# w_down in three loads, two of them into the first 64 partitions, and in front of wo's first half

## The chip, the cores and the metric

The kernel runs on one core of one Trainium2 chip. The time is the device time of one execution in microseconds; a version's time is the median of its runs. Beside it stands one profiled execution, whose trace gives the start and duration of every instruction and the traffic of the 16 DMA engines.

## The reference

One decode step of a gated mixture of two branches, in float32, for a batch of 4 with one token each and a model width of 512:

```python
g = sigmoid((x * gate_w).sum(-1, keepdims=True))
q = (x @ wq) as [4, 32 heads, 128]
p = softmax(q . k_cache / sqrt(128)) over 4096 cached positions
a = (p . v_cache) as [4, 1, 4096] @ wo
b = (gelu(x @ w_gate) * (x @ w_up)) @ w_down
return g * a + (1 - g) * b
```

The caches are [4, 32, 4096, 128] each, 268 MB apiece. The weights are wq [512, 4096], wo [4096, 512], w_gate and w_up [512, 1792], and w_down [1792, 512]. All of it is read once; the output is 8 KB.

## The kernel before, in words

**Attention.** The 128 pairs of batch and head are taken in 32 steps of four heads of one batch entry (`NT`, `HT`). A step's k is one load of 128 partitions by 64 KB, 8.4 MB: a head lies on 32 partitions, each with 128 positions. VectorE (DVE in the profile) multiplies it by the query (`products`, L213) and adds up over the head's width (`sums`, L219), each in a quarter and a three-quarter part. The softmax's maximum goes over TensorE (PE) and ScalarE (ACT) (`max_a`, `soft_max`), and PE multiplies the weights by v in 32 products (`pv`, L272). `gather_a`, `gather`, `weigh`, `turn` and `turned` bring the results of 16 heads into the form that the product with wo wants. wo is used in two halves of 16 heads: the first half's attention is done in the middle of the run, the second's after the last step.

**The feed-forward branch** runs up to its hidden layer at the start (`ffn_up`, `ffn_gelu`, while k's first load is worked on). Its 1792 hidden values are turned into `hT` by 14 transposes (L349), one for each row of w_down that a partition holds: partition p holds the rows 14 p to 14 p + 13, and product i takes row i of all partitions.

**One tile for all that is loaded.** `big` has 45,056 numbers on each of 128 partitions; `place(a, n)` is a piece of it. Two k places overlap by a quarter, and the v place follows them at `VA`. The last v (`V(31)`) is put at 0, into the place of the last but one k. When the steps are over, wo's first half goes to `W0`, the first half of the v place, w_down to `D0`, the second half of it, and wo's second half to `W1`, inside the last k's place. At `ES`, behind wo's second half, small tiles for the last products follow; the last k's place ends 4096 numbers behind `ES`.

**The order.** The program is written in order by hand and each engine takes its instructions in that order. All loads are issued by SyncE (SP) in one queue. SP waits for a load's place to be free: for v's place until `pv` has read it, for k's until `sums` has. A load that waits holds up those behind it in SP's order. Each load counts up one of eight semaphores, which are used in turn. The last loads are, in order: k of step 31, v of step 30, v of step 31, wo's first half (4 MB), w_down (3.5 MB), and wo's second half in four pieces of 9, 4, 2 and 1 sixteenths (`WO_END`).

**The tail.** After the last `pv`, PE multiplies with wo's first half: 16 products into `wide` (`project_wide`, L254), which has four groups of 32 partitions, the products taken in turn; then the 16 transposes of the second half's attention (`turn(1)`, L307) and w_down's 14 products into `wide`. `fold` copies `wide` (ACT, L264) and adds its four groups into `acc`; wo's second half is multiplied into `acc` by 64 products (`project`, L259), four for each sixteenth. `res` is copied from `acc` and stored (L413, L414).

Of the kernel before, what the change touches and what calls it, by code (L numbers as in the profile page):

```python
# [9 lines left out]
F32 = mybir.dt.float32  # L10
# [7 lines left out]
def tile_gated_mix(ctx: ExitStack, tc: tile.TileContext, x, kc, vc, wq, wo, w_gate, w_up, w_down, gate_w, out):  # L18
    nc = tc.nc
    P = 128  # L20
    B, H, S, D = kc.shape
    DM = x.shape[2]
    F = w_gate.shape[1]
# [9 lines left out]
    RJ = 4  # L33
    BP = 2
    FG = F // 4
    FC = F // P
    HW = 16
    E = HW * D // P
    GW = HW // HT
    WO_END = (0, 9, 13, 15, E)  # L40
    scale = 1.0 / math.sqrt(D)
    c_gelu = math.sqrt(2.0 / math.pi)

# [8 lines left out]
    consts = ctx.enter_context(tc.tile_pool(name="consts", bufs=1))  # L52
# [9 lines left out]
    big = kv.tile([P, VA + TW], F32)  # L62
    Q0, F0, F1, W0, D0 = VA, VA, VA + KC * F, VA, VA + TW // 2
    W1, ES = TW, TW + TW // 2

    def place(a, n):
        return big[:, a:a + n]
# [10 lines left out]
    def load_k(i):  # L78
        load_kv(kc, i, K(i))

    def load_v(i):
        load_kv(vc, i, V(i))

    def load_f(s):
        nc.sync.dma_start(place((F0, F1)[s], KC * F), (w_gate, w_up)[s].rearrange("(p c) n -> p (c n)", c=KC))

    def load_d():
        nc.sync.dma_start(place(D0, FC * DM), w_down.rearrange("(p i) n -> p (i n)", i=FC))

    def load_w(w):  # L90
        t = place((W0, W1)[w], E * DM)
        src = wo[w * HW * D:(w + 1) * HW * D].rearrange("(p e) n -> p (e n)", e=E)
        ends = WO_END if w else (0, E)
        for e0, e1 in zip(ends, ends[1:]):
            nc.sync.dma_start(t[:, e0 * DM:e1 * DM], src[:, e0 * DM:e1 * DM])

# [41 lines left out]
    def gates():  # L138
        z = ps2.tile([P, 1], F32, name="sm")
        for c in range(KC):  # L140
            nc.tensor.matmul(z, xT[:, c, :], gw[:, c:c + 1], start=c == 0, stop=c == KC - 1)
        g1 = gate(z)
        z = ps2.tile([P, B], F32, name="sm")
        for c in range(KC):
            nc.tensor.matmul(z, gw[:, c:c + 1].to_broadcast([P, P]), xT[:, c, :32:8], start=c == 0, stop=c == KC - 1)
        g4 = gate(z)

        half = consts.tile([P, 1], F32)
        nc.vector.tensor_scalar(half, g1, -0.5, 0.5, op0=OP.mult, op1=OP.add)
        gmask = consts.tile([P, B, HT], F32)  # L150
        nc.vector.tensor_tensor(gmask, g4[:, :, None].to_broadcast([P, B, HT]), pmask[:, None, :].to_broadcast([P, B, HT]),
                                op=OP.mult)
        return half, gmask
# [5 lines left out]
    for c in range(KC):  # L159
        w = place(Q0 + c * H * D, H * D)  # L160
# [31 lines left out]
    def q_spread(g):  # L192
        ps = ps1.tile([P, B, D], F32, name="q")
        for h in range(HT):
            j, a = divmod(HT * g + h, HG)
            nc.tensor.matmul(ps[h * PH:(h + 1) * PH].rearrange("p b d -> p (b d)"),  # L196
                             hmask[:, j, a:a + 1].to_broadcast([P, PH]), QM.rearrange("p b d -> p (b d)"),
                             start=True, stop=True)
        QB[g] = work.tile([P, B, D], F32, name="qb")
        nc.scalar.activation(QB[g], ps, AF.Copy)  # L200
# [8 lines left out]
    def products(i, shared):  # L209
        g, b = divmod(i, B)  # L210
        r0, r1 = rows(i, shared)
        t = K(i).rearrange("p (r d) -> p r d", d=D)[:, r0:r1]
        nc.vector.tensor_tensor(t, t, QB[g][:, b:b + 1, :].to_broadcast([P, r1 - r0, D]), op=OP.mult)  # L213

    def sums(i, shared):
        if shared:
            SC[i] = work.tile([P, R], F32, name="sc")
        r0, r1 = rows(i, shared)
        nc.vector.tensor_reduce(SC[i][:, r0:r1], K(i).rearrange("p (r d) -> p r d", d=D)[:, r0:r1], axis=AX.X, op=OP.add)  # L219
# [10 lines left out]
    def soft_max(i):  # L230
        g, b = divmod(i, B)
        m2 = work.tile([1, HT], F32, name="m2")
        nc.vector.tensor_reduce(m2, MT[i].rearrange("o (h p) -> o h p", h=HT), axis=AX.X, op=OP.max)  # L233
        nbp = ps2.tile([P, HT], F32, name="sm")
        nc.tensor.matmul(nbp, ones[:1, :], m2, start=True, stop=True)  # L235
        nb = work.tile([P, HT], F32, name="nb")
        nc.scalar.activation(nb, nbp, AF.Copy, scale=-scale)  # L237
        for h in range(HT):
            s = slice(h * PH, (h + 1) * PH)
            nc.scalar.activation(PM[:, PZ:].rearrange("p (c m) -> p c m", m=32)[s, :, h:RJ * HT:HT],  # L240
                                 SC[i][s, :].rearrange("p (c j) -> p c j", j=RJ), AF.Exp, bias=nb[s, h:h + 1], scale=scale,
                                 accum_out=RS[g % 2][s, b, h:h + 1])
# [1 line left out]

    acc = ps1.tile([P, C4], F32, name="acc")
    wide = ps1.tile([P, DM], F32, name="wide")
    NW = FC + E
    nw = iter(range(NW))


    def project_wide(t, w):
        n = next(nw)
        c = n % 4
        nc.tensor.matmul(wide[32 * c:32 * c + 32, :], t, w, start=n < 4, stop=n >= NW - 4)  # L254

# [6 lines left out]
    def fold():  # L262
        t = place(ES + 2 * E * 32, DM)
        nc.scalar.activation(t, wide, AF.Copy)  # L264
        project(stack, t, True, False)
# [13 lines left out]
    def gather_a(i):  # L279
        O[i // BP] = work.tile([P, RJ, D], F32, name="o")  # L280
        nc.scalar.activation(O[i // BP], PO[i // BP % 2], AF.Copy)  # L281
# [27 lines left out]
    def turned(w):  # L309
        t = work.tile([P, E, B * HT], F32, name="tm", bufs=1)  # L310
        nc.vector.tensor_tensor(t, OT[w], gmask.rearrange("p b h -> p (b h)")[:, None, :].to_broadcast([P, E, B * HT]),
                                op=OP.mult)
        nc.vector.tensor_reduce(T1[w], t.rearrange("p e (b h) -> p (e b) h", h=HT), axis=AX.X, op=OP.add)
# [9 lines left out]
    def attended(w, e):  # L323
        return OTS[w][:, e * 32:e * 32 + 32], place((W0, W1)[w] + e * DM, DM)


    hT = consts.tile([P, FC, 32], F32)
    fu = place(VA + 2 * KC * F, 2 * DM).rearrange("p (s n) -> p s n", s=2)

    def ffn_up(s):  # L330
        ps = ps1.tile([P, FG], F32, name="q")
        for c in range(KC):
            for j in range(4):
                nc.tensor.matmul(ps[32 * j:32 * j + 32, :], xT[:, c, :32],  # L334
                                 place((F0, F1)[s] + c * F + j * FG, FG), start=c == 0, stop=c == KC - 1)
        nc.scalar.activation(fu[:, s, :FG], ps, AF.Copy)

    def ffn_gelu():
        x1 = fu[:, 0, :FG]
        t1, t2, t3, th, y, v = (place(F1 + a * DM, FG) for a in range(6))  # L340
        nc.vector.tensor_tensor(t1, x1, x1, op=OP.mult)
        nc.vector.tensor_scalar(t2, t1, 0.044715, 1.0, op0=OP.mult, op1=OP.add)
        nc.vector.tensor_tensor(t3, t2, x1, op=OP.mult)
        nc.scalar.activation(th, t3, AF.Tanh, scale=c_gelu)
        nc.vector.scalar_tensor_tensor(y, th, 1.0, x1, op0=OP.add, op1=OP.mult)  # L345
        nc.vector.scalar_tensor_tensor(v, y, half, fu[:, 1, :FG], op0=OP.mult, op1=OP.mult)  # L346

        for i in range(FC):
            nc.vector.transpose(hT[:, i, :], v[:, i::FC])  # L349

    def ffn_down():
        for f in range(FC):
            project_wide(hT[:, f, :], place(D0 + f * DM, DM))


    load_f(0)
# [2 lines left out]
    for i in range(NT):  # L359
        g, b = divmod(i, B)  # L360
        products(i, True)
        if i > 0:
            soft_max(i - 1)
        if i > B and b == 1 and g % GW == 0:
            turned(g // GW - 1)
        sums(i, True)
        if i < NT - 1:
            load_k(i + 1)
        else:
            load_v(i)  # L370
        products(i, False)
        if i == 0:
            half, gmask = gates()
            ffn_up(0)
            ffn_up(1)
            ffn_gelu()
            load_v(0)
        sums(i, False)
        if i > 0:
            pv(i - 1)  # L380
            if i < NT - 1:
                load_v(i)
            if i % BP == 0:
                gather_a(i - 1)
            if b == 0:
                gather(g - 1)
        max_a(i)
        if i > 0 and b == 0:
            weigh(g - 1)
            if g % GW == 0:  # L390
                turn(g // GW - 1)
        if b == 1 and g + 1 < NG:
            q_spread(g + 1)
    load_w(0)
    load_d()
    load_w(1)
    spread(0)
    soft_max(NT - 1)
# [1 line left out]
    gather_a(NT - 1)  # L400
    gather(NG - 1)
    weigh(NG - 1)
    for e in range(E):
        project_wide(*attended(0, e))
    turn(1)
    turned(1)
    spread(1)
    ffn_down()
    fold()
    for e in range(E):  # L410
        project(*attended(1, e), False, e == E - 1)
# [25 lines left out]
```

## Time and profile before

| | before |
|---|---|
| median of 3 runs | 1314.11 us (1314.06 to 1314.94) |
| profiled execution, its time | 1313.67 us |
| its span, first to last instruction | 1311.9 us |
| DVE busy | 1143.1 us, 87% of the span |
| PE busy | 393.9 us, 30% |
| ACT busy | 92.6 us, 7% |
| HBM read | 564.67 MB, 430 GB/s over the span |
| share of the chain that ended last | DMA 72%, DVE 26%, PE 1% |

All times in the profile count from the first instruction. PE is TensorE's products, PEld its loads of weights, SPq an instruction of SyncE, which issues loads. In the timeline a row is: start, duration, engine, line, operation, output and input tiles, shape, count, and in brackets the engine's idle time before it with what ended it. In the chain a row is: start, duration, what. In the list of issues, a row ends with the size in KB and the microseconds from issue to landing. In the list of SP's waits a row is: who waited for whom, microseconds in total, times, longest. A DMA share of 1.00 means that all 16 DMA engines are busy.

### The profile page before, as it was taken

What the parts mean: (1) busy time and instruction counts of PE and PEld (TensorE: products, weight loads), DVE (VectorE), ACT (ScalarE), POOL (GpSimd) and SP (SyncE); (2) the same over time, 40 slices, a digit from 0 to 9 for tenths busy, and PEclk for the clock granted to TensorE, in tenths of its full rate; (3) what the DMA queues carried; (4) which work ended last, traced back from release to release, by engine and by line L of the source; (5) the groups of instructions that cost most, each with busy time, mean ns of one, the idle gap of its engine ahead of it and who ended that gap; (6) DMA issues with size and microseconds to landing.
All of it is one profiled execution on the core that took longest, in us unless ns stands there. A gap on an engine that the chain in (4) does not pass through costs nothing.

```text
span 1311.9 us, 6362 instructions
## 1 busy us (share of the span) xinstructions
PE 393.9 (30%) x2728; PEld 131.6 (10%) x2728; DVE 1143.1 (87%) x261; ACT 92.6 (7%) x321; POOL 0.7 (0%) x6
## 2 busy tenths in 40 slices
PE   2503233212333321332322332332123323123237
PEld 0201001000011000110001000100001000010013
DVE  1899989988899988988989988998889898898890
ACT  0010000000000100000000000000000000000010
POOL 0000000000000000000000000000000000000000
PEclk9556666556666656666655666665666665566668
DMA  9999999999999999999999999999999999999997
GB/s 416 432 430 444 422 442 422 440 436 436 434 430 436 428 436 440 436 432 430 434 436 434 434 432 436 426 440 434 432 440 426 442 424 440 436 430 442 424 428 341
DMA packets 10711, 565.07 MB, mean 431 GB/s; under 512 B 1320, under 2 KB 1336, under 8 KB 1596
## 3 DMA queue, kind: packets, MB, share of 16 engines
q1 hardware_dynamic: 10684, 564.68, 99.5%
q8 instruction: 21, 0.34, 0.1%
q14 instruction: 6, 0.05, 0.0%
HBM read 564.67 MB, written 0.01 MB: 430 GB/s over the span
## 4 chain that ended last, share of the span: by engine, by line
DMA 72%; DVE 26%; PE 1%; issue 0%; SPq 0%; ACT 0%; DVEq 0%
DMA big<-in_A_k_cache 66%; DVE sc L219 13%; DVE big L213 12%; DMA big<-in_A_wo 2%; DMA big<-in_B_w_up 2%; DMA big<-in_A_x 2%; PE po L164 1%; PE q L334 0%; DVE m L233 0%; DVE hT L349 0%; PE acc L259 0%; DVE m L226 0%; DVE big L346 0%; DVE big L345 0%; PE sm L125 0%
## 5 line engine op out<-in xcount | busy, mean ns | idle before, releaser
L213 DVE TENSOR_TENSOR big<-big,qb 128x4096 f32<-128x4096 f32 x64 | 555.8, 8684 | 103.3 <-DMA big<-in_A_k_cache 103.3
L219 DVE TENSOR_REDUCE sc<-big 128x32 f32<-128x4096 f32 x64 | 555.4, 8678 | 1.1
L272 PE MATMUL po<-big,PM 128*32 128x512 f32 x2048 | 293.2, 737 | 437.1 <-DMA big<-in_A_v_cache 434.7
L272 PEld LDWEIGHTS po<-big,PM 128*32 128x32 f32 x2048 | 80.4, 132 | 623.7 <-issue 621.2
L235 PE MATMUL sm<-m,ones 1*128 1x4 f32 x64 | 18.7, 360 | 217.9 <-DVE m L233 217.9
L228 PE MATMUL sm<-ident,m 128*1 128x128 f32 x32 | 11.8, 368 | 216.6 <-DVE m L226 182.1
L240 ACT ACTIVATE PM<-sc,nb 32x128 f32<-32x128 f32 x128 | 67.4, 527 | 2.6
L237 ACT ACTIVATE nb<-sm 128x4 f32<-128x4 f32 x32 | 5.6, 174 | 573.3 <-PE sm L235 573.3
L235 PEld LDWEIGHTS sm<-m,ones 1*128 1x128 f32 x64 | 15.9, 306 | 237.5 <-DVE m L233 237.5
L281 ACT ACTIVATE o<-po 128x512 f32<-128x512 f32 x16 | 9.6, 597 | 322.1 <-PE po L272 322.1
L228 PEld LDWEIGHTS sm<-ident,m 128*1 128x1 f32 x32 | 2.5, 79 | 239.5 <-issue 185.7
L240 ACT ACTIVATION_READ_ACCUMULATOR PM<-sc,nb 32x1 f32 x128 | 26.2, 205 | 0.0
L200 ACT ACTIVATE qb<-q 128x512 f32<-128x512 f32 x8 | 4.8, 597 | 246.7 <-PE q L196 246.7
L128 DVE COPY xT<-sm 128x128 f32<-128x128 f32 x4 | 0.9, 284 | 20.4 <-PE sm L125 20.4
L196 PE MATMUL q<-QM,hmask 128*32 128x512 f32 x64 | 15.5, 1061 | 3.5 <-DVE QM L186 3.5
L289 PE MATMUL sm<-o,sel 128*16 128x128 f32 x128 | 15.6, 273 | 0.0
L334 PE MATMUL q<-big,xT 128*32 128x448 f32 x64 | 11.5, 897 | 9.1 <-DMA big<-in_B_w_gate 4.9
L299 DVE RECIPROCAL ri<-sm 16x1 f32<-16x1 f32 x8 | 1.2, 147 | 13.9 <-PE sm L291 13.9
L289 PEld LDWEIGHTS sm<-o,sel 128*16 128x16 f32 x128 | 11.7, 97 | 7.4 <-issue 5.0
L413 DVE COPY res<-acc 128x128 f32<-128x128 f32 x1 | 0.3, 291 | 11.8 <-PE acc L259 11.8
L226 DVE TENSOR_REDUCE m<-sc 128x1 f32<-128x128 f32 x32 | 9.2, 286 | 1.1
L164 PE MATMUL po<-big,xT 128*32 128x512 f32 x64 | 9.3, 747 | 0.4 <-DVE xT L128 0.4
(61 smaller groups left out, 78.9 us busy)
## 6 DMA issues: line engine op xcount, KB each, us to landing
big<-in_A_wo SPq DMA_DIRECT2D x1, 4096.0 KB, 23.7
big<-in_B_w_gate SPq DMA_DIRECT2D x1, 3584.0 KB, 20.8
big<-in_B_w_up SPq DMA_DIRECT2D x1, 3584.0 KB, 27.2
big<-in_B_w_down SPq DMA_DIRECT2D x1, 3584.0 KB, 28.8
big<-in_A_wo SPq DMA_DIRECT2D x1, 2304.0 KB, 27.4
big<-in_A_wo SPq DMA_DIRECT2D x1, 1024.0 KB, 29.5
big<-in_A_k_cache SPq DMA_DIRECT2D x32, 29.6
big<-in_A_v_cache SPq DMA_DIRECT2D x32, 29.5
```

Of the source, the lines that this page charges most:

```text
L164: nc.tensor.matmul(PO[s][32 * j:32 * j + 32].rearrange("p j d -> p (j d)"), xT[:, c, :32], w[:, n0:n0 + HB * D], start=c == 0, stop=c == K ...
L196: nc.tensor.matmul(ps[h * PH:(h + 1) * PH].rearrange("p b d -> p (b d)"), hmask[:, j, a:a + 1].to_broadcast([P, PH]), QM.rearrange("p b d ...
L213: nc.vector.tensor_tensor(t, t, QB[g][:, b:b + 1, :].to_broadcast([P, r1 - r0, D]), op=OP.mult)
L219: nc.vector.tensor_reduce(SC[i][:, r0:r1], K(i).rearrange("p (r d) -> p r d", d=D)[:, r0:r1], axis=AX.X, op=OP.add)
L226: nc.vector.tensor_reduce(m1, SC[i], axis=AX.X, op=OP.max)
L228: nc.tensor.transpose(MT[i], m1, ident)
L235: nc.tensor.matmul(nbp, ones[:1, :], m2, start=True, stop=True)
L240: nc.scalar.activation(PM[:, PZ:].rearrange("p (c m) -> p c m", m=32)[s, :, h:RJ * HT:HT], SC[i][s, :].rearrange("p (c j) -> p c j", j=RJ) ...
L272: nc.tensor.matmul(PO[i // BP % 2][32 * c:32 * c + 32].rearrange("p j d -> p (j d)"), PM[:, m0:m0 + 32], V(i)[:, j * N:(j + 1) * N], start ...
L281: nc.scalar.activation(O[i // BP], PO[i // BP % 2], AF.Copy)
L289: nc.tensor.matmul(OS[g][:, :D], sel[:, j, m0:m0 + B * HT], O[N * g + n][:, j, :], start=(n, j) == (0, 0), stop=(n, j) == (N - 1, RJ - 1))
L334: nc.tensor.matmul(ps[32 * j:32 * j + 32, :], xT[:, c, :32], place((F0, F1)[s] + c * F + j * FG, FG), start=c == 0, stop=c == KC - 1)
```

## The change

w_down's load is cut into three. The first brings 12 of each partition's 14 rows to the old place. The remaining two rows of the partitions 0 to 63 are a load of 64 rows of 1024 numbers (4 KB) into partitions 0 to 63, and those of the partitions 64 to 127 another load of the same shape into the same 64 partitions, behind the first. In the source the 64 rows are grouped as eight by eight. Both go to the last 2048 numbers of the last k's place (`DX`). The two rows' hidden values are transposed into `hX`, on 64 partitions, in four transposes in place of two, and w_down's products are 12 over 128 partitions and four over 64.

w_down is loaded in front of wo's first half, and that half comes in two loads. PE takes w_down's products first, then the transposes, then those of wo's first half.

```diff
-    FC = F // P
+    FR = F // P
+    XR = 2
+    FC = FR - XR
+    XP, XC = P // 2, 2 * XR
...
-    WO_END = (0, 9, 13, 15, E)
+    WO_END = ((0, E // 2, E), (0, 9, 13, 15, E))
...
+    DX = ES + 4 * DM
...
     def load_d():
-        nc.sync.dma_start(place(D0, FC * DM), w_down.rearrange("(p i) n -> p (i n)", i=FC))
+        rows = w_down.rearrange("(p i) n -> p i n", i=FR)
+        nc.sync.dma_start(place(D0, FC * DM), rows[:, :FC].rearrange("p i n -> p (i n)"))
+        for k in range(2):
+            nc.sync.dma_start(place(DX + k * XR * DM, XR * DM)[:XP],
+                              rows[k * XP:(k + 1) * XP, FC:].rearrange("(a p) i n -> a p (i n)", p=8))
...
-        ends = WO_END if w else (0, E)
+        ends = WO_END[w]
...
-    NW = FC + E
+    NW = FC + XC + E
...
+    hX = consts.tile([XP, XC, 32], F32)
...
         for i in range(FC):
-            nc.vector.transpose(hT[:, i, :], v[:, i::FC])
+            nc.vector.transpose(hT[:, i, :], v[:, i::FR])
+        for k in range(2):
+            for i in range(XR):
+                nc.vector.transpose(hX[:, k * XR + i, :], v[k * XP:(k + 1) * XP, FC + i::FR])
...
     def ffn_down():
         for f in range(FC):
             project_wide(hT[:, f, :], place(D0 + f * DM, DM))
+        for f in range(XC):
+            project_wide(hX[:, f, :], place(DX + f * DM, DM)[:XP])
...
+    load_d()
     load_w(0)
-    load_d()
     load_w(1)
...
-    for e in range(E):
-        project_wide(*attended(0, e))
+    ffn_down()
     turn(1)
     turned(1)
     spread(1)
-    ffn_down()
+    for e in range(E):
+        project_wide(*attended(0, e))
     fold()
```

## The prediction

> **What bounds the kernel now.** I read the page first (busy shares, the row of DMA shares, the chain by line), then the chain in order of time for the last 110 us, the timeline of the last 60 us, SP's issues with their time to landing, and the windows of the last five microseconds.
>
> ```profile
> span 1311.9 us, 6362 instructions
> ...
> DMA  9999999999999999999999999999999999999997
> ...
> DMA 72%; DVE 26%; PE 1%; issue 0%; SPq 0%; ACT 0%; DVEq 0%
> ...
> 40.00:1300.00 1260.00, 374.21 (x2496) 124.29 (x2500) 1134.88 (x237) 90.10 (x318) 0.00 (x0) 0.62 1.00 433
> ```
>
> The last line is a window: busy time of PE, PEld, DVE, ACT and POOL, then the granted clock, the DMA share and GB/s. From 40 to 1300 us the 16 DMA engines are busy at a share of 1.00 and move 433 GB/s. The DVE (87% of the span) follows them. Only what adds bytes, slows the stream, lets it run dry or changes how it ends can move the time. One DMA engine carries 433 / 16 = 27.1 GB/s.
>
> ```profile
> 1277.25 30.31 DMA big<-in_A_wo
> 1307.56 0.04 issue
> 1307.60 1.06 PE acc L259 x24
> 1308.66 0.02 issue
> 1308.68 0.29 DVE res L413
> ```
>
> The chain's end: from wo's second half, through the last products into `acc`, a copy (0.3) and the store. The end is set by when wo's last pieces land, plus some 1.1 us of PE.
>
> ```profile
> 1231.49 19.38 SPq L76 DMA_DIRECT2D big<-in_A_v_cache  x2
> ...
> 1266.14 0.33 SPq L95 DMA_DIRECT2D big<-in_A_wo  x1
> 1269.54 0.33 SPq L88 DMA_DIRECT2D big<-in_B_w_down  x1
> 1276.40 1.75 SPq L95 DMA_DIRECT2D big<-in_A_wo  x4
> ...
> big<-in_A_wo SPq DMA_DIRECT2D x1, 4096.0 KB, 23.7
> big<-in_B_w_down SPq DMA_DIRECT2D x1, 3584.0 KB, 28.8
> ...
> big<-in_A_wo SPq DMA_DIRECT2D x1, 256.0 KB, 30.4
> big<-in_A_v_cache SPq DMA_DIRECT2D x1, 29.6
> ```
>
> Issue plus time to landing: the last v load at 1250.5 + 29.6 = 1280.1, wo's first half at 1266.1 + 23.7 = 1289.8, w_down at 1269.5 + 28.8 = 1298.3, wo's last piece at about 1277.7 + 30.4 = 1308.1. The gaps are 9.7, 8.5 and 9.8 us for 4.19, 3.67 and 4.19 MB, each at about 430 GB/s: one unbroken stream in the order of issue, every load issued 10 to 30 us ahead.
>
> ```profile
> 1303.50:1304.50 1.00, 0.30 (x12) 0.25 (x14) 0.00 (x0) 0.60 (x1) 0.00 (x0) 1.00 0.65 270
> 1304.50:1305.50 1.00, 1.00 (x48) 1.00 (x42) 0.00 (x0) 0.00 (x0) 0.00 (x0) 1.00 0.55 225
> 1305.50:1306.50 1.00, 1.00 (x48) 1.00 (x40) 0.00 (x0) 0.00 (x0) 0.00 (x0) 1.00 0.55 213
> 1306.50:1307.50 1.00, 1.00 (x40) 0.74 (x28) 0.00 (x0) 0.00 (x0) 0.00 (x0) 1.00 0.24 94
> 1307.50:1308.50 1.00, 0.91 (x26) 0.53 (x24) 0.00 (x0) 0.00 (x0) 0.00 (x0) 1.00 0.03 12
> ```
>
> The engines don't end together: the share is 0.65, 0.55, 0.55, 0.24, 0.03. About half of them are out of work by 1305 and the other half runs on to about 1307.5. Levelled perfectly, the five windows' work (shares sum to 2.02 us) would end at 1305.5: no levelling can bring more than some 2.4 us. The views don't say which engines are late.
>
> **The change part by part.**
>
> *Two of w_down's rows.* Of 14 rows of 2 KB per partition, 12 keep their place (128 partitions, 3.15 MB). The other two (524,288 bytes) come in two loads of 64 rows of 4 KB into partitions 0 to 63. No bytes are added. Spread over 16 engines at full rate they take 524,288 / 433 GB/s = 1.21 us, as before: 0. Where they would take longer is that only half the partitions are written. No load of the trace writes 64 partitions; every large one writes 128, and whatever its size each moves at 27.1 GB/s for each eight partitions. If that rate goes with the partitions, 64 of them take 217 GB/s: 2.42 us, +1.21 on all engines. The other end is a gain: if the two loads ran on eight engines only and these were the early eight, those would get 65,536 bytes in place of 32,768 (+1.21 us) and the late eight 32,768 fewer (-1.21). So the bounds are -1.2 and +1.2.
>
> In the source the 64 rows are written as eight by eight, but they lie evenly apart, and the built program names one run of 64 rows of 1024 numbers on both sides; nothing in the instruction says eight. I therefore take 16 engines writing 64 partitions, and, as the nearest rows are the 128-partition loads with their fixed rate for each eight partitions, the half rate: **+1.2 us**.
>
> [...]
>
> *Three more loads in the stream* (two of w_down's, one from wo's first half cut in two). The last 4.19 MB came in four pieces and took 9.8 us against 9.7 for wo's first half in one: three cuts, **+0.1 us**, between 0 and 0.2.
>
> *The order, and SP's queue.* w_down's 12 rows go where the last v's second half lay, free at the same moment as before (1269.5); wo's first half, issued at 1266.1 until now, stands behind it. The two new loads go to the end of the last k's place and wait for its sums, the wait that wo's second half had (SP free at 1276.4). Behind them now stand both halves of wo: eight issues. At 0.44 us each (1.75 for four) they are out by 1279.9, at the store's 0.66 by 1281.7.
>
> ```profile
> 1309.00 0.66 SPq L414 DMA_DIRECT2D out<-res  x1
> ...
> SPq L95 <- DVE m L226: 6.8, 1, 6.8
> ...
> SPq L433 <- DMA out<-res: 1.1, 1, 1.1
> ```
>
> The cover is v until 1280.1 and 3.15 MB of w_down (7.3 us) until 1287.4, so 5.7 us are left: 0. Had SP's wait lasted 6 us longer, each further microsecond would cost one. The program also makes the third and fourth piece of wo's second half wait for an earlier load (the last v, 1280.1, and w_down's 12 rows, 1287.4), as its eight load semaphores go round; the pieces run after 1308: 0.
>
> *PE.* Landings would be: w_down's 12 rows 1287.4, its rest 1289.8, wo's first half 1294.7 and 1299.5, the second half's pieces 1305.0, 1307.4, 1308.6 and 1309.3.
>
> ```profile
> 1291.23 3.60 PE L254 MATMUL wide<-big 128*32 128x512 f32 x29
> ...
> 1294.76 1.16 PE L307 MATMUL oT<-ident,ONA 16*128 16x16 f32 x16
> ...
> 1298.40 5.15 PE L254 MATMUL wide<-big,hT 128*32 128x512 f32 x28 [2.48 <-DMA big<-in_B_w_down]
> ...
> 1303.60 0.60 ACT L264 ACTIVATE big<-wide 128x512 f32<-128x512 f32 x1 [6.10 <-PE wide L254]
> 1304.25 0.43 PE L259 MATMUL acc<-big,stack 128*32 128x128 f32 x8 [0.70 <-ACT big L264]
> ...
> 1304.49 4.12 PE L259 MATMUL acc<-big 128*32 128x128 f32 x128
> 1307.60 0.38 PEld L259 LDWEIGHTS acc<-big 128*32 128x32 f32 x16 [0.35 <-DMA big<-in_A_wo]
> ```
>
> w_down's 16 products (two more, as the moved rows need four of 64 partitions for two of 128) start at 1291.2 with all landed and take wo's 3.7 us: 1294.9. The transposes (1.2) end at 1296.1, wo's first eight products (1.8) at 1297.9; the second eight wait for 1299.5 and end at 1301.3; the copy (0.6) and the fold (0.4) end near 1302.5. The second half's first 36 products wait for 1305.0, and the last four for 1309.3, where they waited for 1308.1 before. So the stream decides as it did: 0; what a low clock would add is a rival.
>
> *DVE at the start.* Four half-height transposes in place of two full ones: two more at 1.71 / 14 = 0.12 us.
>
> ```profile
> 68.91 1.71 DVE L349 STREAM_TRANSPOSE hT<-big 128x32 f32<-128x32 f32 x14
> ...
> 70.76 0.33 SPq L76 DMA_DIRECT2D big<-in_A_v_cache  x1
> ...
> 75.00:80.00 5.00, 0.00 (x0) 0.00 (x0) 5.00 (x1) 0.00 (x0) 0.00 (x0) 0.50 1.12 485
> ```
>
> The first v load waits for them and goes out 0.24 us later, while k, issued at 51, keeps the engines full past 75 (share 1.12): 0.
>
> **Sum.** 1.2 + 0.1 = +1.3 us on the profiled execution's 1313.67 (span 1311.9 and 1.8 around it): 1315.0. The median of the runs is 0.44 above that execution, 1314.11, which makes **1315.4**, 0.1% above. From no change, a measurement of this kernel can tell some 0.2%, 2.6 us, so the forecast is "no change".
>
> **Rivals.**
>
> *The half rate doesn't come* (0.20): all engines take their 32,768 bytes at 27.1 GB/s. [...] +0.1 gives 1314.2.
>
> *The levelling works* (0.22): the two loads run on the eight early engines, which end near 1306.6, and the late ones end 1.2 earlier. For it: half of the engines do run dry early, and 2 x 1.21 us is close to their distance. Against: the folded 64 rows. 1314.11 - 1.2 + 0.1 = 1313.0. If the eight were the late ones (0.06), +1.3: 1315.4.
>
> *PE's clock* (0.04, the other side).
>
> ```profile
> 1298.00:1299.00 1.00, 0.60 (x4) 0.20 (x8) 0.00 (x0) 0.00 (x0) 0.00 (x0) 0.55 0.94 406
> ...
> 1301.00:1302.00 1.00, 1.00 (x12) 0.28 (x8) 0.00 (x0) 0.00 (x0) 0.00 (x0) 0.75 0.92 389
> ```
>
> After 2.5 us without work (up to 1298.4) the granted clock was 0.55 and came back within 1301 to 1302; after 0.7 us (1304.25) it was 1.00. Now PE may stand idle from 1302.5 to 1305.0. The first 52 products (pieces one and two) took 2.8 us from 1304.5 until PE waited for the third piece: 0.053 each. At half the clock throughout, 64 products take 6.8 us from 1305.0 and end at 1311.8, where the stream alone gives 1309.8: +2.0, 1317.4, slower by 0.25%. With the low clock for 3.3 us as at 1298, 31 products are done in it and the other 33 in 1.75: 1310.1, +0.3, which lies in the forecast's own range. It decides if the clock stays low for over 5 us.
>
> *The stream drains at each 64-row load* (0.05, the other side): the store of 8 KB, issued at 1309.0, is still unfinished near 1310.8, some 1.8 us; two loads that must land alone cost 3.6: 1317.8, slower by 0.28%. It decides as soon as the engines stand idle behind one load. Against it, small loads early in the program left no gap:
>
> ```profile
> 22.00:40.00 18.00, 11.84 (x76) 3.02 (x76) 6.14 (x14) 0.60 (x1) 0.00 (x0) 0.87 1.03 444
> ```
>
> **How the numbers follow.** The half rate has 0.41, the two rivals that leave 1314.2 and 1313.0 have 0.20 and 0.22, the late eight 0.06, the clock 0.04, draining 0.05; 0.02 is left for a gain I don't see. The range runs from 1312.7 (levelling, less 0.3 for the runs' scatter) to 1316.5 (the half rate, +0.3 of clock and 0.8 for scatter and small terms) and leaves out about 0.11; cases of both signs are in it, and the forecast's own range is 1314.8 to 1316.2. Faster by over 0.2% needs a gain larger than all levelling gives: 0.02. Slower by over 0.2%: draining 0.05 and the low clock 0.04, 0.09 in all. The rest is 0.89.
>
> **What would show it.** In the profile after: w_down's first load lands near 1287.4; between 1287 and 1292 (about) the GB/s dip to half for some 2.4 us or the late engines run longer; the last wo piece lands near 1309.3; the share's fall at the end begins later and ends later. Levelling would show as a share near 1.0 until 1305 and a steep fall by 1307. No gap in SP's issues reaches the stream. The prediction is wrong if the last landing comes before 1307.5, or if the last products are held by PE and not by wo.

## The result, and the profile after

The changed kernel takes 1318.99 us, median of 5 runs (1318.45 to 1319.52), against 1314.06 us for the kernel before on the same chip: a ratio of 1.0037, 95% interval 1.0026 to 1.0049, or 3.4 to 6.4 us. It is slower by more than the 0.2% that can be told from no change. Run again later beside one of the experiments, against 1313.78, it took 1318.84: 1.0037 (1.0024 to 1.0050). The forecast was 1315.4, range 1312.7 to 1316.5: the time lies 2.5 us above the range.

The profiled execution took 1319.52 us, its span is 5.8 us longer than before. The page after, and the windows after, around the place of w_down's small loads and at the end (columns as in the prediction: PE, PEld, DVE, ACT, POOL, granted clock, DMA share, GB/s):

```profile
span 1317.7 us, 6376 instructions
...
DMA 71%; DVE 28%; PE 0%; issue 0%; SPq 0%; ACT 0%; DVEq 0%
```

```profile
1281.00:1283.00 2.00, 2.00 (x12) 0.39 (x8) 0.00 (x0) 0.00 (x0) 0.00 (x0) 0.50 0.93 369
1283.00:1285.00 2.00, 2.00 (x16) 0.47 (x12) 0.00 (x0) 0.00 (x0) 0.00 (x0) 0.50 1.03 238
1285.00:1287.00 2.00, 2.00 (x24) 0.56 (x20) 0.00 (x0) 0.00 (x0) 0.00 (x0) 0.88 1.02 297
1287.00:1289.00 2.00, 2.00 (x24) 0.53 (x20) 0.00 (x0) 0.00 (x0) 0.00 (x0) 1.00 1.02 236
1289.00:1291.00 2.00, 2.00 (x22) 1.05 (x15) 0.00 (x0) 0.60 (x1) 0.00 (x0) 1.00 1.04 213
1291.00:1293.00 2.00, 2.00 (x22) 1.07 (x24) 0.89 (x2) 0.00 (x0) 0.00 (x0) 1.00 0.97 250
1293.00:1295.00 2.00, 2.00 (x24) 0.45 (x16) 0.00 (x0) 0.00 (x0) 0.00 (x0) 1.00 0.96 369
...
1283.00:1295.00 12.00, 12.00 (x106) 4.13 (x98) 0.89 (x2) 0.60 (x1) 0.00 (x0) 0.90 1.01 267
...
1295.00:1305.00 10.00, 6.34 (x52) 2.07 (x48) 0.84 (x2) 0.63 (x1) 0.00 (x0) 0.83 1.00 429
...
1307.00:1309.00 2.00, 0.00 (x0) 0.00 (x0) 0.00 (x0) 0.00 (x0) 0.00 (x0) 1.00 0.75 308
1309.00:1311.00 2.00, 1.70 (x34) 1.65 (x38) 0.00 (x0) 0.00 (x0) 0.00 (x0) 0.60 0.51 210
1311.00:1313.00 2.00, 2.00 (x48) 1.94 (x44) 0.00 (x0) 0.00 (x0) 0.00 (x0) 0.55 0.26 100
1313.00:1314.00 1.00, 1.00 (x48) 1.00 (x40) 0.00 (x0) 0.00 (x0) 0.00 (x0) 1.00 0.01 4
```

The same 12 us before, from its windows:

```profile
1283.00:1295.00 12.00, 12.00 (x110) 4.38 (x102) 0.89 (x2) 0.60 (x1) 0.00 (x0) 0.94 1.00 430
```

The chain's shares still say DMA: the loss is in the stream. From 1283 to 1293 the engines are busy (share 0.97 to 1.04), and move little more than half of what they did. (430 - 267) GB/s over 12 us are 1.96 MB not moved, 4.6 us at 430 GB/s. Behind 1295 the rate is back at 429. The dip holds nearly 4 times what the forecast gave it. The two small loads are only 0.52 MB, and 267 GB/s over 12 us are 3.2 MB: so most of the traffic in the dip is that of other loads.

The trace also keeps the size and the duration of every DMA packet (a piece of a load, here one row of it on one partition), which no view prints one by one. In these microseconds a packet of the two small loads has 4 KB, one of w_down's 12 rows 24 KB, and one of wo's first half 16 KB. Undisturbed, as in the first experiment below, they take 159, 912 and 611 ns, with one exception among the last. In the changed kernel the small ones took 283 ns in the mean, and single packets of 24 and 16 KB up to 1802 and 1852 ns. The time above the undisturbed durations, added up and divided by 16 engines, is 1.0 us in the two small loads, 1.2 us in w_down's 12 rows and 2.5 us in wo's first half: 4.7 us, which agrees with the dip's 4.6. So the engines were held longer by the same bytes, and nearly four fifths of the loss fell on the loads around.

SP's timeline, its wait behind line 104, and the list of issues after:

```profile
1276.44 1.19 SPq L96 DMA_DIRECT2D big<-in_B_w_down  x2
1277.67 13.52 SPq L104 DMA_DIRECT2D big<-in_A_wo  x6
```

```profile
SPq L104 <- DMA big<-in_B_w_down: 10.3, 1, 10.3
```

```profile
big<-in_B_w_down SPq DMA_DIRECT2D x1, 3072.0 KB, 21.6
...
big<-in_B_w_down SPq DMA_DIRECT2D x2, 256.0 KB, 17.4
...
big<-in_A_wo SPq DMA_DIRECT2D x1, 256.0 KB, 22.7
```

wo's last piece waits 10.3 us in SP for w_down's landing (1269.25 + 21.6 = 1290.9) and is the last of the six issues, which end at 1277.67 + 13.52 = 1291.2; 22.7 us from 1290.9 it lands near 1313.5, where it was 1308.1 before. The chain's end and PE's timeline after:

```profile
1278.78 30.48 DMA big<-in_A_wo
1309.30 5.41 PE acc L268 x128
```

```profile
1291.72 0.63 PE L263 MATMUL wide<-big,hT 128*32 128x512 f32 x3
...
1294.44 1.09 PE L263 MATMUL wide<-big,hX 64*32 64x512 f32 x8
...
1299.02 3.58 PE L263 MATMUL wide<-big 128*32 128x512 f32 x16 [2.40 <-DMA big<-in_A_wo]
1303.85 1.92 PE L263 MATMUL wide<-big 128*32 128x512 f32 x16 [1.26 <-DMA big<-in_A_wo]
...
1309.30 5.36 PE L268 MATMUL acc<-big 128*32 128x128 f32 x128 [2.38 <-DMA big<-in_A_wo]
```

The first piece of wo's second half lands at 1309.3, 4.3 us later than forecast. PE then runs without a break, by the last windows above at a granted clock of 0.55 to 0.60 until about 1313, and takes 5.36 us for the 64 products that took 4.12 before, waits for wo's last pieces included. So this execution has two losses: a large one in the stream near 1283 to 1294, and a small one in PE behind it.

### The profile page after: what moved, and what is told of

Its sections match the earlier page's. It is cut to its first block, busy times and chain, and to the rows that moved or that the text cites. A ratio compares the mean times of both kernels' runs of the same rounds, so it can differ in the third digit from the quotient of the medians.

```text
span 1317.7 us, 6376 instructions
## 1 busy us (share of the span) xinstructions
PE 398.4 (30%) x2732; PEld 133.2 (10%) x2732; DVE 1143.6 (87%) x263; ACT 92.6 (7%) x321; POOL 0.7 (0%) x6
## 2 busy tenths in 40 slices
DMA packets 11015, 565.07 MB, mean 429 GB/s; under 512 B 1368, under 2 KB 1384, under 8 KB 1772
## 4 chain that ended last, share of the span: by engine, by line
DMA 71%; DVE 28%; PE 0%; issue 0%; SPq 0%; ACT 0%; DVEq 0%
DMA big<-in_A_k_cache 68%; DVE big L222 14%; DVE sc L228 14%; DMA big<-in_A_wo 2%; PE acc L268 0%; DVE m L242 0%; DVE hT L359 0%; SPq L104 0%; DVE m L235 0%; SPq L96 0%; DVE big L356 0%; DVE big L353 0%; DVE big L351 0%; DVE big L355 0%; ACT big L354 0%
## 6 DMA issues: line engine op xcount, KB each, us to landing
big<-in_B_w_down SPq DMA_DIRECT2D x1, 3072.0 KB, 21.6
```

## The experiments

How many engines carry a load is read here from the page's count of packets under 512 B:

```profile
DMA packets 10711, 565.07 MB, mean 431 GB/s; under 512 B 1320, under 2 KB 1336, under 8 KB 1596
...
DMA packets 10855, 565.07 MB, mean 431 GB/s; under 512 B 1336, under 2 KB 1352, under 8 KB 1612
```

The first line is the kernel before, the second that with the order alone, which has one load more: 16 packets of 4 bytes more, read here as one from each engine of that load. The changed kernel has 1368, three loads on 16 engines more. But no view of the profile names the engine or the partition of a packet. What the theories say of the partitions that an engine writes, in the ordinary loads of 128 partitions and in the others, is therefore the author's assumption, tried on how the time answers to edits. Letters in the expectations stand for theories, which they give in words. One row of the windows is shown for each kernel, always 1283 to 1295; 430 GB/s is the row before.

**One load of 128 partitions, and the order alone.** The first kernel keeps the order, but brings the two rows in one load of 128 partitions:

```diff
-    XP, XC = P // 2, 2 * XR
+    XP, XC = P, XR
...
-        for k in range(2):
-            nc.sync.dma_start(place(DX + k * XR * DM, XR * DM)[:XP],
-                              rows[k * XP:(k + 1) * XP, FC:].rearrange("(a p) i n -> a p (i n)", p=8))
+        nc.sync.dma_start(place(DX, XR * DM), rows[:, FC:].rearrange("p i n -> p (i n)"))
```

> The two rows come in one load of 128 partitions by 4 KB, from the same 4-KB pieces of w_down; order and products' total stay as in the changed kernel. Theory A (the changed kernel loses about 5 us because its two loads write only the first 64 partitions, which slows every engine while they are under way): the stretch from 1283 to 1294 moves at 420 to 435 GB/s again and the time is within 1 us of before, 1313.5 to 1315. Theory B (the 4-KB pieces, 28 KB apart in memory, are slow to read, wherever they are written): the dip to 220 to 300 GB/s stays and the time is 1318 to 1319.5. Theory C (the order of w_down and wo): 1318 to 1319.5, with or without the dip.

The second has the loads of the kernel before, w_down in 14 rows, and changes only the order, with wo's first half in two loads.

```diff
-    load_w(0)
     load_d()
+    load_w(0)
```

> The kernel before with the order alone changed: w_down in one load in front of wo's first half, that half in two loads, PE's products in the new order. Theory A and theory B: no loss, 1313.5 to 1315. Theory C: the greater part of the 4.9 us, 1317 to 1319.5.

Measured against 1313.85: 1314.26 (1.0002, 0.9992 to 1.0011) with one load of 128, and 1314.46 (1.0006, 0.9997 to 1.0015) with the order alone. Their rows, one load of 128 first (the second's 416 comes with a share of 0.97):

```profile
1283.00:1295.00 12.00, 12.00 (x100) 4.30 (x94) 0.89 (x2) 0.60 (x1) 0.00 (x0) 0.87 1.00 427
```

```profile
1283.00:1295.00 12.00, 12.00 (x109) 4.56 (x101) 0.89 (x2) 0.60 (x1) 0.00 (x0) 0.95 0.97 416
```

No dip, so neither the order, nor rows of 4 KB, nor a small load in the stream is the cause; the two loads of 64 rows are. What the order does cost shows in the chain of the second kernel:

```profile
1276.34 27.60 DMA big<-in_A_wo
1303.98 5.41 PE acc L259 x128
```

The first piece is there at 1303.9, where the forecast had it without the half rate (1305.0 less 1.2). PE takes 5.41 us from there, and the copy to `res` begins at 1309.4 against 1308.68 before: 0.7 us, which go with a low clock (0.50 from 1305 to 1307, 0.74 from 1307 to 1309) and which the timed runs can't tell from nothing.

**Which partitions, and how many engines.** The third kernel puts the second load of 64 rows into partitions 64 to 127. The fourth writes the source so that it can't be folded into one run of 64, to get eight engines; the count of packets (1352, that is 16 + 2 x 8 more than before) agrees with that.

```diff
-            nc.sync.dma_start(place(DX + k * XR * DM, XR * DM)[:XP],
+            nc.sync.dma_start(place(DX, XR * DM)[k * XP:(k + 1) * XP],
```

> Two loads of 64 rows as in the changed kernel, but the second goes into partitions 64 to 127. Theory A in the form that each load alone crowds its half: the dip stays in depth and length, 1317.5 to 1319.5. Theory A in the form that the sum over the first half counts (16 engines' bytes into 64 partitions, twice): about half of the loss is left, 1315.5 to 1317. Theory B: 1318 to 1319.5.

```diff
-                              rows[k * XP:(k + 1) * XP, FC:].rearrange("(a p) i n -> a p (i n)", p=8))
+                              rows[k * XP:(k + 1) * XP, FC:].rearrange("(p a) i n -> a p (i n)", p=8))
```

> As the changed kernel, but the 64 rows are taken from w_down in another order, which cannot be folded into one run, so that the load's source has eight by eight rows in the program too; the output is not the reference's, as w_down's last two rows meet the wrong hidden values. If the source's outer count decides how many engines carry a load, eight carry these two. Theory A (crowding of 16 engines on half the partitions): with eight engines there is little crowding, the dip is mostly gone; if the eight are the early ones the fall of the DMA share at the end is steeper and the time is 1312.5 to 1314, if they are the late ones 1315 to 1316. If the outer count decides nothing: as the changed kernel, 1318 to 1319.5. Theory B: 1318 to 1319.5.

Measured: 1318.6 (1.0034, 1.0021 to 1.0047) and 1319.02 (1.0035, 1.0023 to 1.0048). Both halves, then eight engines:

```profile
1283.00:1295.00 12.00, 12.00 (x117) 4.94 (x109) 0.89 (x2) 0.60 (x1) 0.00 (x0) 0.99 0.99 300
```

```profile
1283.00:1295.00 12.00, 11.84 (x102) 3.94 (x94) 0.90 (x2) 0.60 (x1) 0.00 (x0) 0.96 1.01 284
```

Both pay in full, +4.8 and +5.2 us. A side of the partitions that is written twice isn't the cause, and the levelling that a grouping in eights might have brought doesn't come.

**32 rows, on eight engines and on 16.** Now the two rows come in four loads of 32 rows, into partitions 0 to 31. In the first kernel the source is grouped as eight by four and can't be folded; in the second it is one run of 32. Nothing else differs.

```diff
-    XP, XC = P // 2, 2 * XR
+    XP, XC = P // 4, 4 * XR
...
-    DX = ES + 4 * DM
+    DX, DY = ES + 4 * DM, VA + TW // 2 + FC * DM
+    DXS = (DX, DX + XR * DM, DY, DY + XR * DM)
...
-        for k in range(2):
-            nc.sync.dma_start(place(DX + k * XR * DM, XR * DM)[:XP],
-                              rows[k * XP:(k + 1) * XP, FC:].rearrange("(a p) i n -> a p (i n)", p=8))
+        for k in range(4):
+            nc.sync.dma_start(place(DXS[k], XR * DM)[:XP],
+                              rows[k * XP:(k + 1) * XP, FC:].rearrange("(p a) i n -> a p (i n)", a=8))
```

> The same two rows of w_down in four loads of 32 rows of 4 KB, each into the first 32 partitions, the source eight by four so that eight engines carry each load, four partitions an engine (the output is not the reference's: rows and hidden values don't match, and the last two loads' products use the first two's hidden values). Theory P (a load that writes fewer than 128 partitions slows the stream): a dip as in the changed kernel or deeper, 1318 to 1320. Theory Q (it is not how many partitions, but that an engine writes partitions which it doesn't write in the 128-partition loads): here each of the eight may write four of its own, no dip, 1313.5 to 1315.5. Theory I (the longer form of issue): a dip, 1318 or more.

```diff
-                              rows[k * XP:(k + 1) * XP, FC:].rearrange("(p a) i n -> a p (i n)", a=8))
+                              rows[k * XP:(k + 1) * XP, FC:].rearrange("p i n -> p (i n)"))
```

> As the run before, but the source is a plain run of 32 rows, which 16 engines carry, two partitions each; the program issues it in its short form (the output is not the reference's: the last two loads' products use the first two's hidden values). Theory P: a dip, 1318 to 1320. Theory Q: a dip, 1317 to 1320. Theory I: no dip, as the form is the short one, 1313.5 to 1315.5.

Measured against 1313.76: 1314.76 (1.0004, 0.9994 to 1.0014) and 1318.54 (1.0037, 1.0024 to 1.0050). Eight by four, then one run:

```profile
1283.00:1295.00 12.00, 12.00 (x110) 4.29 (x106) 0.90 (x2) 0.60 (x1) 0.00 (x0) 0.93 1.00 425
```

```profile
1283.00:1295.00 12.00, 12.00 (x114) 4.20 (x106) 0.89 (x2) 0.60 (x1) 0.00 (x0) 0.97 1.01 274
```

The counts, 1368 and 1400, are those of four loads on eight and on 16 engines. In the first kernel each of the 128 small packets took 159 ns, in the second 271 ns in the mean. This overturns the forecast's reason: loads that write a quarter of the partitions cost nothing that can be told from no change, and the same bytes to the same partitions, grouped in another way, cost 4.8 us. The grouped source also takes longer to issue at SP (2.96 us for the four loads, where those of one run took 1.72), so that had to be taken apart from it.

**The form of the issue, and 128 partitions grouped in another way.** Both start from the kernel with one load of 128 partitions. The first issues it in the longer form. The second groups the source as 16 by 8, meant to let each of 16 engines write eight neighbouring partitions; whether it does, no view shows.

```diff
+        nc.dge_precook = False
         nc.sync.dma_start(place(DX, XR * DM), rows[:, FC:].rearrange("p i n -> p (i n)"))
+        nc.dge_precook = True
```

> The kernel with the two rows in one load of 128 partitions (1314.3 us), that load issued in the longer form that the 64-row loads have (0.6 us at SP in place of 0.4). Theory P: no dip, 1313.5 to 1315.5. Theory I: the dip of the changed kernel, 1317 to 1319.5. Theory Q: no dip, unless the longer form gives the rows to the engines in another order.

```diff
-        nc.sync.dma_start(place(DX, XR * DM), rows[:, FC:].rearrange("p i n -> p (i n)"))
+        nc.sync.dma_start(place(DX, XR * DM), rows[:, FC:].rearrange("(p a) i n -> a p (i n)", a=16))
```

> One load of 128 partitions, but the source is sixteen by eight rows that can't be folded, 16 engines (the output is not the reference's, as w_down's last two rows meet the wrong hidden values). Theory P: no dip, 1313.5 to 1315.5. Theory Q: if each engine then takes eight neighbouring partitions, a dip, 1317 to 1320. Theory I: a dip, 1317 to 1320.

Measured: 1314.3 (1.0004, 0.9995 to 1.0013) and 1317.9 (1.0030, 1.0018 to 1.0042). The longer form, then 16 by 8:

```profile
1283.00:1295.00 12.00, 12.00 (x100) 4.30 (x94) 0.89 (x2) 0.60 (x1) 0.00 (x0) 0.87 1.01 431
```

```profile
1283.00:1295.00 12.00, 12.00 (x105) 4.34 (x98) 0.89 (x2) 0.60 (x1) 0.00 (x0) 0.94 1.00 291
```

The form does nothing. And a load of all 128 partitions pays 4.1 us, nearly as much as those of 64, with its rows grouped otherwise; both kernels have 16 engines for it by the count (1352). So the number of partitions is out from both sides.

**Half the bytes.** One row instead of two comes in 64-row loads (13 rows stay in the large load); beside it the changed kernel ran again.

```diff
-    XR = 2
+    XR = 1
```

> [...] If the price went with the fewer partitions alone as predicted (1.2 us for two rows): 1314.5 to 1315.3.

> The changed kernel once more, beside the half of it on the same chip: 1318 to 1319.5 by every theory. Its profile shows whether depth and length of the dip repeat: 1283 to 1294, 200 to 300 GB/s.

Measured against 1313.78: 1316.2 (1.0018, 1.0009 to 1.0028), +2.4, and 1318.84, +5.1. One row:

```profile
1283.00:1295.00 12.00, 12.00 (x104) 4.16 (x96) 0.89 (x2) 0.60 (x1) 0.00 (x0) 0.99 1.00 348
```

(430 - 348) x 12 us are 0.98 MB, half of the 1.96 MB with two rows, and the time agrees. With the rows grouped alike, in two loads both times, the price went with the bytes, not with the number of loads. The dip is some 8 us long (1283 to 1291, 278 to 336 GB/s), where that of two rows was some 10 (1283 to 1293, 213 to 297).

The changed kernel's second profile repeats the dip, and its chain ends otherwise:

```profile
1283.00:1295.00 12.00, 12.00 (x106) 4.08 (x98) 0.89 (x2) 0.60 (x1) 0.00 (x0) 0.99 1.00 273
...
1280.27 32.41 DMA big<-in_A_wo
1312.68 0.04 issue
1312.73 0.64 PE acc L268 x16
1313.37 0.00 issue
1313.37 0.47 PE acc L268 x8
1313.84 0.02 issue
1313.87 0.29 DVE res L428
```

Here PE's granted clock is 1.00 from 1309 on, the products wait for wo's last piece as they did before, and that piece lands at 1312.68 against 1307.56 before, 5.1 us later. So the stream alone makes the 5 us; the low clock at the end is not in every execution.

**The same grouping, other partitions.** The last two leave the grouping of eight by four as it is and move only the destination: to partitions 32 to 63, and to 64 to 95.

```diff
+    X0, X1 = 32, 32 + P // 4
...
-            nc.sync.dma_start(place(DXS[k], XR * DM)[:XP],
+            nc.sync.dma_start(place(DXS[k], XR * DM)[X0:X1],
```

> As the four loads of 32 rows on eight engines (four partitions per engine, partitions 0 to 31: no dip, +1.0), but written to partitions 32 to 63. As there, the products take wrong hidden values or rows for the moved rows. Theory Q (what counts is whether an engine writes partitions that it also writes in the loads of 128): only if engines 0 to 7 also write 32 to 63 in those loads is there no dip. [...] Rival R (each engine writes one run of eight neighbouring partitions in the loads of 128, so that partitions 32 to 63 are those of engines 4 to 7): a dip to 220 to 300 GB/s, +4 to +5 us. Rival K (four neighbouring partitions per engine on eight engines is what is free, wherever they lie): no dip.

> The same four loads of 32 rows on eight engines, four partitions per engine, written to partitions 64 to 95. As there, the products take wrong hidden values or rows for the moved rows. Theory Q: the eight engines now write partitions that the other eight write in the loads of 128: dip to 220 to 300 GB/s between 1283 and 1293, median +4 to +5 us, 1317.8 to 1319. Rival K (form of the load alone: eight engines with four neighbouring partitions each): no dip, within 1.5 us of before. Rival R (runs of eight neighbouring partitions) also says a dip here.

Measured against 1313.77: 1314.75 (1.0002, 0.9993 to 1.0012) and 1320.43 (1.0046, 1.0029 to 1.0062). At 32 to 63, then at 64 to 95:

```profile
1283.00:1295.00 12.00, 12.00 (x107) 4.23 (x103) 0.89 (x2) 0.60 (x1) 0.00 (x0) 0.91 1.01 428
```

```profile
1283.00:1295.00 12.00, 11.42 (x106) 4.01 (x98) 0.89 (x2) 0.60 (x1) 0.00 (x0) 0.97 1.00 254
```

Only the destination differs, by 32 partitions; the source, the order of its rows and the count of packets (1368 in each) are the same. It decides: nothing that can be told at 0 to 63 (all small packets at 159 ns), and at 64 to 95 the full price and more, +6.7 us where +4 to +5 was expected. "Eight engines with four neighbouring partitions each are free" falls, and so does "each engine's ordinary partitions are eight neighbours". Nor does the half of the partitions decide alone, since the 64 rows in eight by eight, by the count on eight engines too, paid 5.2 us at 0 to 63. What decides is grouping and destination together: of the variants with two rows, one load of 128 in a plain run cost 0.4 us, 0.5 in the longer form, and the 32 rows of eight by four at 0 and at 32 cost 1.0 each, none of which can be told from no change; every other cost from 4.1 to 6.7.

Of the theories Q is left, by which a load costs when its engines write partitions that other engines write in the ordinary loads. It isn't refuted, but no run shows it: which partitions any engine writes stands in no view. Nor does it say how much is paid: the packets' surplus is 4.7 us in the changed kernel and 4.9 at 64 to 95.

## Why the prediction was wrong, point by point

- **What bounds the kernel**: right. The stream sets the end, and only what slows it moved the time by more than the runs' scatter.
- **Two of w_down's rows, +1.2**: this step failed, in its reason and in what it left out. "If that rate goes with the partitions" is refuted: loads of 32 partitions cost nothing or 4.8 us, by how their rows were grouped, and one of 128 cost 4.1; no run shows the 217 GB/s. The 16 engines agree with the count (1368), but what decided was how the rows were grouped and where they went. The size was worked out for the 0.52 MB of the two loads alone, and there it came near, for a reason that doesn't hold: their own packets lost 1.0 us. The loads around them, put at nothing without a reason, lost 3.7 us more. The bounds of -1.2 and +1.2 were too narrow because both assumed that a load can only slow itself. An estimate from the packets' mean is 16 x 4096 B / 283 ns = 232 GB/s for the two loads, near the forecast's 217; but the load of 128 partitions in 16 by 8, with 255 ns, was at 257 by the same estimate, so inside this stream the number of partitions doesn't decide.
- **Three more loads, +0.1, and the order, 0**: right within the measurement; the order alone was 1.0006 (0.9997 to 1.0015), and its first piece landed where the sum had it.
- **SP's queue, 0**: right in effect, wrong in its times. The eight issues were not out by 1281.7 but by 1291.2, since the last piece's wait for w_down's 12 rows, which the forecast names, lasted 10.3 us; those rows were themselves in the dip (landing 1269.25 + 21.6 = 1290.9 instead of 1287.4). It cost nothing that the windows show: the share stays at 1.00 from 1295 to 1305.
- **PE, 0**: off by 0.7 in the first profile. The rival of PE's clock (0.04) came true in part: products at 0.55 to 0.60 for some 3.5 us, 5.36 us instead of 4.12, in the order alone as well (5.41). With it came one of the forecast's signs of being wrong, the last products held by PE and not by wo; in the second profile they were held by wo, at a clock of 1.00. It was rightly priced between +0.3 and +2.0, and wrongly given a chance of its own beside the forecast: it adds to it.
- **DVE at the start, 0**: nothing contradicts it; no run tests it alone.
- **Levelling (0.22)**: it didn't come. Two loads on eight engines each, by the count (1352), lost as much (1.0035). **Draining (0.05)** gave nearly the right time (1317.8) for a wrong reason: the engines didn't stand idle in the dip, their share was 0.97 or more from 1283 to 1293.

Put together, in the first profile the copy to `res` begins 6.06 us later than before (1314.74 against 1308.68): 0.74 as in the kernel with the order alone, whose clock was low too, and 5.32 from the first piece's later landing (1309.30 against 1303.98). The dip's missing bytes are 4.6 of these 5.3, and the packets' surplus is 4.7. The rest, some 0.6 or 0.7, isn't assigned.

## What to carry to other kernels

In a stream that keeps all DMA engines busy, don't ask only how many partitions or engines a small load uses, but how its rows are grouped at the source and into which partitions they go: the same 0.52 MB in four loads of 32 rows cost 1.0, 4.8 or 6.7 us here by these two alone. A tile that was split or regrouped fell into this silently: only the source's grouping differs between the load of 128 that cost 0.4 us and the one that cost 4.1. Why, no view shows directly; theory Q is what these runs leave standing. The loads around paid with it, and the whole was some four times the small loads' own time (4.6 us for 1.2 us of bytes). Look for a stretch with a DMA share of 1.0 and a low GB/s, as the 1.01 at 267 GB/s here: the engines were busy in it, and the stream was not full. Where a shape can't be kept, try another destination or grouping and compare this one row.

## What the runs showed of the hardware

- Two small loads of 64 rows brought the whole stream from 430 to between 213 and 297 GB/s while they were under way, though the engines showed as busy (0.97 to 1.04). One row cost 2.4 us, two rows 5.1.
- In every kernel that loads the two rows apart and cost nothing, all packets of 4 KB took 159 ns and those of 24 KB 912 ns; in the kernels that paid for two rows the means were 253 to 289 and 1025 to 1099 ns.
- The place decided by itself: the same four loads cost 1.0 us at partitions 0 to 31 and at 32 to 63, with no packet of theirs slowed, and 6.7 us at 64 to 95.
- The small loads' packets overlap with those of the loads around: in the changed kernel they run from 1282.4 to 1293.0, w_down's 24-KB packets until 1289.9, and wo's 16-KB packets from 1284.2. All three sorts are slowed then, and in the experiment with one load of 128, with the like overlap (small packets from 1282.6, 24-KB ones until 1287.2), none of the first two is. Why a packet is slowed then is open, as no view shows the engines apart.
- After 2.4 us without work PE's granted clock was 0.55 to 0.60 for some 3.5 us (first profile after), and 0.55 after 2.5 us in the profile before. In the second profile after, PE waited for wo's pieces 0.66 us at most and the clock in the tail was 1.00.
